# Scores of the attention blocks as one matmul of 64 rows by 128 columns in place of four of 64 by 32

## The chip, the cores and the metric

The kernel runs on one core of one Trainium2 chip. The metric is the device time of one execution in microseconds (us). A change is called faster or slower in this document where it moves the time by more than 0.2%.

## The reference

A transformer layer with attention and a dense block side by side. x is 2048 tokens of 512, float32.

```
xn  = layernorm(x)
q, k, v = split(xn @ wqkv)                    # 32 heads of 16
o   = softmax(q @ k.T / 4) @ v                # per head, 2048 x 2048 scores
out = x + o @ wo + gelu(xn @ w1 + b1) @ w2 + b2     # w1 is 512 x 1792
```

## The kernel before

**Stages.** A prologue (to about 87 us) normalizes x, turns it, and makes q and k of the first eight heads, most of v, and the scores of the first 19 units. Its order on every engine is set by a small planner (`Plan`). Then the block loop runs (to about 1425 us): 512 units, a unit being four heads, 512 queries and 128 keys. A short tail finishes the output.

**A unit** has two halves, `a` = 0 and 1 in `unit` (L819). In each half TensorE gets, in this order:

- two products of *transposed scores* (`e_half`, L432, tile pT: keys x queries) and two of *scores* (`s_half`, L405, tile pS: queries x keys), in the order pT, pS, pS, pT. One pT and one pS use rows 0 to 63 of the array, the other two rows 64 to 127, since a head's q and k are stacked with their low halves into 64 rows (62 used for the scores). Each product is of 64 rows by 128 columns of weights, and 512 columns of moving operand. ScalarE takes the exponential of pT (`pe`, L443). VectorE takes the row maxima of pS (`mt`, L402), which are needed for blocks to come: after the 16 units of a stretch they are turned by two matmuls of 64 rows by 32 columns (`m_turn`, L378), go to memory and come back as two more rows of the stacked q;
- four matmuls with v (`v_half`, L446, tile pV), float32, 64 rows by 32 columns each, one per head, in one half of the array's rows;
- three or four *dense* products (tile pD) in the other half of the rows: projections, the two layers of the dense block and the output projection, cut into such pieces. `dense` hands them out, and their number per half comes from a pace per group (`FAST`, `MEAN`, `SLOW`).

The next half swaps the halves of the rows. Scores run 19 units ahead of the transposed scores (`LEAD`).

**How a product becomes matmuls.** `tiled` (L202) cuts the 128 columns of weights of a score, transposed score or dense product into pieces of `wide[0]` columns, each written to its own 32 partitions of the PSUM bank. `wide[0]` is 128 while the prologue's plan is made, and 32 after that, so the block loop's pieces are all of 64 rows by 32 columns. `user` is "D" for dense products of the block loop, and None for scores. Dense products that take a score's place in the last 19 units (`Halves`, L767) pass None too. The matmuls with v call `product` without `tiled`. Where the array is used whole (prologue, tail), `nc.tensor.matmul` is called directly.

**Order.** The block loop's order on each engine is the order in which the code issues it. PSUM has three banks for pS, three for pT, one each for pV and pD.

Of the kernel before, what the change touches and what calls it, by code (L numbers as in the profile page):

```python
# [18 lines left out]
P = 128  # L19
# [26 lines left out]
VT = 2600, -8000  # L46
WV_TAIL, WV_DVE = 56000, 2
FINE = "fine"
ORDERED = {mybir.EngineType.SP, mybir.EngineType.PE, mybir.EngineType.Activation, mybir.EngineType.DVE, mybir.EngineType.Pool}
GELU_C = 0.7978845608028654  # L50
GELU_A = 0.044715
# [7 lines left out]
def layer_kernel(ctx: ExitStack, tc: tile.TileContext, x, wqkv, wo, w1, b1, w2, b2, out):  # L59
# [68 lines left out]
    def scales(am, n, bank, box):  # L128
# [9 lines left out]
        nc.vector.tensor_scalar(c[:, :n], pb[:, :n], 2.0 ** -100, 2.0 ** 100, op0=ALU.max, op1=ALU.min)  # L138
        yield FINE
        fac = const.tile([P, n], F32, name=f"fac{len(made)}")  # L140
        inv = const.tile([P, n], F32, name=f"inv{len(made)}")
        made.append(fac)
        nc.vector.tensor_single_scalar(fac.bitcast(I32), c[:, :n].bitcast(I32), 0x7F800000, op=ALU.bitwise_and)
        yield FINE
        nc.vector.reciprocal(inv, fac)
# [26 lines left out]
    def product(user, *args, **kw):  # L172

        p = nc.tensor.matmul(*args, **kw)  # L174
        if user is None:
            return
        if user in goal:
            p._wait_ge(turns[user], counted[user])
            tc.declare_fence(p.ins, group=goal.pop(user))
        newest[user] = p  # L180
# [19 lines left out]
    wide = [32]  # L200

    def tiled(user, dst, lhs, rhs, start, stop):  # L202

        for j in range(0, P, wide[0]):
            product(user, dst[j:j + wide[0]], lhs[:, j:j + wide[0]], rhs, start=start, stop=stop)


    scale_of, wfs = {}, []
# [177 lines left out]
    def s_mm(u, n, s):  # L386

        t, i = divmod(u, 16)
        g, qb = divmod(t, NQB)
        qt, kb = divmod(i, 4) if t else (i % 4, i // 4)  # L390
        ks, qs = kst[g % 2], qst[g % 2]
        p, a = divmod(n, 2)
        r = slice(64 * a, 64 * a + 62)
        tiled(None, s, qs[qb][r, p, P * qt:P * qt + P], ks[kb][r, p, :], True, True)
# [37 lines left out]
    def e_half(u, n):  # L432

        p, a = divmod(n, 2)
        t, kt = divmod(u, 16)
        g, qb = divmod(t, NQB)
        st = banks("T")
        r = slice(64 * a, 64 * a + 64)
        k0 = (kt % 4) * P
        tiled(None, st, kst[g % 2][kt // 4][r, p, k0:k0 + P], qst[g % 2][qb][r, p, :], True, True)  # L440
        pe = work.tile([P, QB], F32, name="pe", bufs=12)
        ptiles[u, n] = pe
        nc.scalar.activation(pe, st, AF.Exp, scale=scale_of[g // 2])  # L443
        given("act", 520)
# [131 lines left out]
    class Group:  # L576
# [15 lines left out]
        def product(self, side):  # L592

            if self.bank is None:
                self.bank, self.key = self.alloc()
            lhs, rhs = self.prods[side % 2][self.at[side % 2]]()
            start = self.first and self.at == [0, 0]
            if side == 2:
                self.at = [min(self.at[0] + 1, n) for n in self.n]
                nc.tensor.matmul(self.bank, lhs, rhs, start=start, stop=self.last and self.over())  # L600
                return
            r = slice(64 * side, 64 * side + 64)
            self.at[side] += 1
            tiled("D", self.bank, lhs[r], rhs[r], start, self.last and self.over())
# [34 lines left out]
    def by_slots(gen):  # L639

        def step():
            w = FINE
            while w == FINE:
                w = next(gen, 0)
            if w is None:
                later(1, step, True)
# [226 lines left out]
    with ExitStack() as st1:  # L873
# [40 lines left out]
        loads, fac_v, ready_w = [None] * NM, [], {}  # L914
        ctx.enter_context(tc.manual_schedule(engines=ORDERED))
        plan = Plan(xs=8, xp=8, stg=3, pf=2, wch=3, wq=2, S=4, X=4)
# [354 lines left out]
        for n, src in enumerate(every[:NM]):  # L1271
            key = ("wch", "m", n)
            dst = am_all[:, 12 + n:13 + n] if n < 2 else am_all[:, n - 2:n - 1] if n < 9 else amx[:, n - 2:n - 1]
# [346 lines left out]
```

## Time and profile before

| | us |
|---|---|
| median of 3 runs | 1438.83 (1438.03 to 1439.07) |
| the profiled execution | 1438.07 |
| its span, first to last instruction | 1436.3 |
| TensorE busy, 39979 matmuls | 1423.7 |
| weight loads busy, 39979 | 969.1 |
| VectorE busy | 1346.9 |
| ScalarE busy | 1253.5 |
| GpSimd busy | 693.4 |

Engines are named PE (matmuls), PEld (weight loads, which can run beside matmuls), DVE (VectorE), ACT (ScalarE), POOL (GpSimd) and SP. In a row of the timeline stand the start, the time from the first start to the last end, the engine, the line, the operation, the tiles out<-in, the shapes and the number of records that are merged. A record of a matmul is modelled from its start and its size, so that the next may start well before it ends: steps are read from start to start. The four strips of one product are four records that overlap. The granted clock of TensorE is 1.00 throughout.

### The profile page before, as it was taken

The page shows a single profiled execution, that of the slowest core. Times are in us where ns is not written, and L with a number is a line of the kernel's source. Part 1 is how long each engine was busy: PE and PEld are TensorE (multiplying, and loading weights), DVE is VectorE, ACT ScalarE, POOL GpSimd, SP SyncE. Part 2 cuts the span into 40 slices and gives each one's busy share as a digit, 9 for nine tenths or more (in the row PEclk, how much of TensorE's full clock was granted, in tenths as well). Part 3 has the DMA queues.
Part 4 walks back from the last instruction along what each step waited for, and adds up shares of the span by engine and source line. Part 5 has one row for each costly group of instructions (what it writes and reads, how often), then busy time and mean ns, then how long its engine had stood idle before and what let it go on. Part 6 is the DMA issues. An engine that isn't in the chain of part 4 may idle for free.

```text
span 1436.3 us, 88274 instructions
## 1 busy us (share of the span) xinstructions
PE 1423.7 (99%) x39979; PEld 969.1 (67%) x39979; DVE 1346.9 (94%) x2239; ACT 1253.5 (87%) x2389; POOL 693.4 (48%) x780
## 2 busy tenths in 40 slices
PE   8999999999999999999999999999999999999998
PEld 4657777666667777666667766676666667666665
DVE  8989999999999999999999999999999999999943
ACT  6678888889999888999988899998889998888886
POOL 6203866665687311478831157783026787202210
PEclk9999999999999999999999999999999999999999
DMA  7733556455224111221122011122112110212323
GB/s 233 225 114 97 162 158 206 158 172 148 85 65 128 60 27 27 64 76 43 38 59 75 25 51 45 52 71 60 38 32 77 57 39 19 60 56 78 109 73 116
DMA packets 110784, 124.95 MB, mean 87 GB/s; under 512 B 20812, under 2 KB 82252, under 8 KB 110408
## 3 DMA queue, kind: packets, MB, share of 16 engines
q1 hardware_dynamic: 103208, 109.87, 25.1%
q10 hardware_dynamic: 7200, 9.44, 2.2%
q8 instruction: 312, 5.11, 1.5%
q14 instruction: 64, 0.52, 0.1%
HBM read 81.79 MB, written 37.34 MB: 83 GB/s over the span
## 4 chain that ended last, share of the span: by engine, by line
PE 90%; DVE 5%; DMA 2%; issue 2%; ACT 1%; POOL 0%; SPq 0%; DVEq 0%; ACTq 0%; POOLq 0%
PE pD L174 28%; PE pV L174 26%; PE pT L174 19%; PE pS L174 16%; DVE mt L402 3%; DMA wch<-in_B_w_dram 1%; DMA pe<-in_A_x_dram 0%; DVE bs L1011 0%; DMA qk_d<-stg 0%; DMA wq<-in_A_wqkv_dram 0%; DMA wch<-in_A_wo_dram 0%; DVE ac L1493 0%; PE pD L1074 0%; ACT pe L443 0%; DVE wvh L1196 0%
## 5 line engine op out<-in xcount | busy, mean ns | idle before, releaser
L402 DVE TENSOR_REDUCE mt<-pS 128x1 f32<-128x512 f32 x2029 | 1279.1, 683 | 34.7 <-PE pS L174 8.2
L443 ACT ACTIVATE pe<-pT 128x512 f32<-128x512 f32 x2048 | 1109.4, 599 | 141.0 <-PE pT L174 60.2
L174 PE MATMUL pV<-pe,vv 64*32 64x512 f32 x8192 | 1086.6, 591 | 0.1
L174 PE MATMUL pT<-qst,kst 64*32 64x512 f16 x8192 | 703.4, 378 | 0.6 <-ACT vv L1212 0.3
L174 PE MATMUL pS<-kst,qst 62*32 62x512 f16 (+1 forms) x7945 | 627.0, 378 | 1.3 <-issue 0.8
L174 PEld LDWEIGHTS <-qst 62*32 62x32 f16 (+1 forms) x7964 | 309.9, 91 | 186.0 <-issue 34.1
L174 PE MATMUL pD<-xb,wc 64*32 64x512 f16 x5376 | 363.3, 375 | 0.0
L174 PE MATMUL pD<-w_s,g 64*32 64x512 f16 x5376 | 361.1, 375 | 0.0
L174 PEld LDWEIGHTS <-kst 64*32 64x32 f16 x8192 | 281.3, 91 | 98.5 <-issue 24.4
L174 PEld LDWEIGHTS pV<-pe,vv 64*32 64x32 f32 x8192 | 241.5, 105 | 11.0 <-PE pV L174 2.3
L174 PEld LDWEIGHTS <-wc 64*32 64x32 f16 x5376 | 160.4, 91 | 45.2 <-issue 0.3
L174 PEld LDWEIGHTS <-g 64*32 64x32 f16 x5376 | 162.6, 91 | 38.8 <-POOL g L1408 0.3
L174 PE MATMUL pD<-xt,wqk_h 64*32 64x512 f16 x2400 | 160.0, 376 | 0.1
L372 POOL TENSOR_SCALAR mparts<-mx 128x16 f16<-128x16 f32 x32 | 6.6, 206 | 294.3 <-DVE mx L370 284.6
L1460 POOL TENSOR_TENSOR xa<-xa,yt 128x512 f32<-128x512 f32 x16 | 20.6, 1284 | 167.8 <-ACT yt L1458 167.8
L174 PEld LDWEIGHTS <-wqk_h 64*32 64x32 f16 (+1 forms) x2448 | 78.2, 92 | 20.3 <-issue 1.0
L1414 POOL TENSOR_TENSOR t<-t,hh 128x512 f32<-128x512 f32 x56 | 71.9, 1284 | 4.7
L1407 POOL TENSOR_TENSOR t<-t,hh 128x512 f32<-128x512 f32 x56 | 71.8, 1283 | 4.5
L1412 POOL TENSOR_TENSOR t<-hh 128x512 f32<-128x512 f32 x56 | 58.3, 1041 | 21.3 <-ACT hh L1435 18.9
L1409 POOL TENSOR_TENSOR g<-t,g 128x512 f16<-128x512 f32 x56 | 65.2, 1165 | 4.7
L174 PE MATMUL pD<-wo_s,oc 64*32 64x512 f16 x912 | 61.0, 376 | 0.3 <-issue 0.3
L513 POOL TENSOR_TENSOR osb<-osb,rb 128x512 f32<-128x512 f32 x31 | 39.9, 1286 | 42.3 <-DMA rb<-den_d 29.0
(170 smaller groups left out, 942.1 us busy)
## 6 DMA issues: line engine op xcount, KB each, us to landing
wc<-w_d SPq DMA_DIRECT2D x56, 256.0 KB
qk_d<-stg SPq DMA_DIRECT2D x32, 256.0 KB
rb<-den_d SPq DMA_DIRECT2D x124, 64.0 KB
wch<-in_B_w_dram ACTq DMA_DIRECT2D x14, 512.0 KB
wch<-in_B_w_dram SPq DMA_DIRECT2D x28, 256.0 KB
w_d<-wsp SPq DMA_DIRECT2D x28, 256.0 KB
kst<-qk_d SPq DMA_DIRECT2D x64, 96.0 KB
qst<-qk_d SPq DMA_DIRECT2D x64, 96.0 KB
```

The costliest lines, as they stand in the source:

```text
L174: p = nc.tensor.matmul(*args, **kw)
L372: lambda: nc.gpsimd.tensor_scalar(parts[:, :, 0], mx[:, 0], 1.0 / MROW, 0.0, op0=ALU.mult, op1=ALU.add),
L402: nc.vector.reduce_max(mt_of[t][:, n // 2 + n % 2 * 2, qt, kb:kb + 1], s, axis=AX.X)
L443: nc.scalar.activation(pe, st, AF.Exp, scale=scale_of[g // 2])
L513: pooled((1280, lambda: nc.gpsimd.tensor_tensor(osb, osb, rb, op=ALU.mult)), (620, lambda: nc.gpsimd.tensor_scalar(ot[:, 0], osb, 1.0, 0.0 ...
L1407: (1280, lambda: nc.gpsimd.tensor_tensor(t1, t1, hh, op=ALU.mult)),
L1409: (1160, lambda: nc.gpsimd.tensor_tensor(g[:, 1, f, :], t1, g[:, 0, f, :], op=ALU.subtract)),
L1412: pooled((1040, lambda: nc.gpsimd.tensor_tensor(t1, hh, hh, op=ALU.mult)), (620, lambda: nc.gpsimd.tensor_scalar(t1, t1, 1.0, 1.0 / GELU_A ...
L1414: (1280, lambda: nc.gpsimd.tensor_tensor(t1, t1, hh, op=ALU.mult)),
L1460: add = lambda: nc.gpsimd.tensor_tensor(xa, xa, yt, op=ALU.add)
```

## The change

`tiled` takes the larger of `wide[0]` and an entry for the user. Scores and transposed scores (user None) thus become one matmul of 64 rows by 128 columns in the block loop as well; dense products ("D") and those with v keep 32.

```diff
+WIDE = {None: 128}
...
     def tiled(user, dst, lhs, rhs, start, stop):
 
-        for j in range(0, P, wide[0]):
-            product(user, dst[j:j + wide[0]], lhs[:, j:j + wide[0]], rhs, start=start, stop=stop)
+        n = max(wide[0], WIDE.get(user, 0))
+        for j in range(0, P, n):
+            product(user, dst[j:j + n], lhs[:, j:j + n], rhs, start=start, stop=stop)
```

Lines after the first addition move by one, those after `tiled` by two. On VectorE, ScalarE, GpSimd and SP the instructions stand in the same order as before. On TensorE the same products stand in the same order, with fewer instructions.

TensorE before, the end of a dense group's products and the scores of a half in the middle of the block loop (each row of the scores stands there four times; kst and qst are the stacked k and q, wc is a part of w1, xb of the normalized x):

```order
L174 MATMUL pD_22326<-xb_15758,wc_21822 32x512
...
L174 LDWEIGHTS kst1_3_86
L174 MATMUL pT_22390<-qst1_1_92,kst1_3_86 32x512
...
L174 LDWEIGHTS qst1_3_94
L174 MATMUL pS_22397<-kst1_0_83,qst1_3_94 32x512
...
L174 MATMUL pS_22404<-kst1_0_83,qst1_3_94 32x512
...
L174 MATMUL pT_22410<-qst1_1_92,kst1_3_86 32x512
L174 MATMUL pV_21341<-pe_22252,vv_95 32x512
```

TensorE after, at such a place of the block loop (32x512 and 128x512 are partitions and columns of the result):

```order
L175 MATMUL pD_15833<-xb_12170,wc_15466 32x512
L175 LDWEIGHTS kst1_3_86
L175 MATMUL pT_15885<-qst1_0_91,kst1_3_86 128x512
L175 LDWEIGHTS qst1_1_92
L175 MATMUL pS_15889<-kst1_3_86,qst1_1_92 128x512
L175 LDWEIGHTS qst1_1_92
L175 MATMUL pS_15892<-kst1_3_86,qst1_1_92 128x512
L175 LDWEIGHTS kst1_3_86
L175 MATMUL pT_15895<-qst1_0_91,kst1_3_86 128x512
L175 MATMUL pV_15174<-pe_15777,vv_95 32x512
```

Sixteen pairs of a weight load and a matmul have become four, and every half now goes from 32 columns to 128 and back. The instructions of TensorE are 64460 rows before and 40034 after.

TensorE after, where the row maxima of a stretch are turned (mparts are the maxima, nident the negative identity), in the scores of the second half of a stretch's first unit:

```order
L175 MATMUL pS_2258<-kst0_0_79,qst0_2_89 128x512
L380 LDWEIGHTS mparts_2209
L380 MATMUL pT_2261<-nident_98,mparts_2209 32x64
...
L175 LDWEIGHTS kst0_3_82
L175 MATMUL pT_2269<-qst0_0_87,kst0_3_82 128x512
L175 MATMUL pV_1415<-pe_2176,vv_95 32x512
```

The two turning matmuls keep 32 columns; before, their neighbours had 32 as well, now they stand between matmuls of 128. There are 32 such places, the first of them in the prologue, where the neighbours had 128 already. In the whole program the pieces of successive matmuls go from 64x128 to 64x32 1058 times (twice before), and from 64x32 to 64x128 1056 times (once before).

## The prediction

> **What bounds the kernel now.** I read the page first (engines, then the chain that ended last), then the groups of instructions with their shapes kept apart, then single stretches of the timeline.
>
> ```profile
> PE 1423.7 (99%) x39979; PEld 969.1 (67%) x39979; DVE 1346.9 (94%) x2239; ACT 1253.5 (87%) x2389; POOL 693.4 (48%) x780
> PE 90%; DVE 5%; DMA 2%; issue 2%; ACT 1%; POOL 0%; SPq 0%; DVEq 0%; ACTq 0%; POOLq 0%
> ```
>
> TensorE is busy 99% of the span and 90% of the chain runs through it. Work per time there is the question, and busy shares don't answer it, since eight matmuls run beside each other. So I count half units. A half unit is one turn of the inner loop of `unit`: two products of scores, two of transposed scores, then four matmuls with v beside three or four dense products. The group of the matmuls with v, taken from 200 to 1400 us alone, gives the period:
>
> ```profile
> L174 PE MATMUL pV<-pe,vv 64*32 64x512 f32 x7384 | 979.6, 591 | 0.1
> ```
>
> Each of the four matmuls of a half leaves two records (float32 goes through in two passes), so 7384 records are 923 halves in 1200 us: 1.300 us per half. There are 1024 halves in the kernel (512 blocks, two each), 1331 us of the 1438.
>
> What is in a half? Two stretches of the timeline. The shape after the operands is rows*columns of the weights, then of the moving operand; the second number is the time from the first start to the last end of the merged records.
>
> ```profile
> 77.86 0.37 PE L174 MATMUL pD<-wvh,xt 64*128 64x512 f16 x1
> 77.89 0.37 PE L174 MATMUL pT<-wvh,xt 64*128 64x512 f16 x1
> 78.07 0.37 PE L174 MATMUL pD<-wvh,xt 64*128 64x512 f16 x1
> ...
> 78.29 0.38 PE L174 MATMUL pD<-wvh,xt 64*128 64x512 f16 x1
> 78.32 0.37 PE L174 MATMUL pT<-wvh,xt 64*128 64x512 f16 x1
> 78.62 0.20 PE L378 MATMUL pS<-nident,mparts 64*32 64x64 f16 x2
> 78.76 0.61 PE L174 MATMUL pT<-wvh,xt 64*128 64x512 f16 x4
> 701.41 0.61 PE L174 MATMUL pV<-pe,vv 64*32 64x512 f32 x3
> ...
> 701.84 0.60 PE L174 MATMUL pV<-pe,vv 64*32 64x512 f32 x3
> ```
>
> The first stretch is of the prologue, where scores and v tiles are already made by weights of 64 rows by 128 columns. In one half of the rows a 512-column fp16 matmul follows the other after 0.215 us (77.86, 78.07, 78.29), while the other half of the rows runs its own. A pass with v takes 0.43 us (701.41 to 701.84). A half of the block loop therefore streams for at least 2 x 0.215 + 2 x 0.43 = 1.29 us where the matmuls with v stand. It takes 1.300. TensorE streams back to back, whatever the number of instructions that carry the stream. VectorE stands close behind:
>
> ```profile
> 62.52 1.88 DVE L402 TENSOR_REDUCE mt<-pS 128x1 f32<-128x512 f32 x3
> 64.31 0.68 DVE L402 TENSOR_REDUCE mt<-pV 128x1 f32<-128x512 f32 x1
> 575.79 12.14 DVE L402 TENSOR_REDUCE mt<-pS 128x1 f32<-128x512 f32 x20
> ```
>
> Unhindered, a row maximum follows the last one after 0.60 us (62.52 to 64.31 is three; twenty at 575.79 are as tight). Two of them per half make 1.20 us, the lowest that a half can come to whatever happens on TensorE.
>
> **The change part by part.** It removes, in each half, 12 of the 16 weight loads and 12 of the 16 matmuls of scores; no column of the stream goes away, because four matmuls over four strips of 32 columns run beside each other and stream as long as one over 128. What the fewer instructions save is bounded by what the weight loads of scores waited for "issue", the time for which the profile shows no cause:
>
> ```profile
> L174 PEld LDWEIGHTS <-qst 62*32 62x32 f16 x7888 | 304.4, 91 | 181.4 <-issue 33.1
> L174 PEld LDWEIGHTS <-kst 64*32 64x32 f16 x8192 | 281.3, 91 | 98.5 <-issue 24.4 <-DMA qst<-m_d 0.7
> ```
>
> That is 33.1 + 24.4 = 57.5 us at most, and nothing at least. I take nothing, because the half already stands 0.01 us above its stream.
>
> What it adds is a change of the array's division. Before, everything in the block loop used pieces of 64 rows by 32 columns. Now each half goes from 64x32 (v and dense) to 64x128 (scores) and back: two changes in each of 1024 halves. The trace of before shows that very pair once each way, in the rows at 78.32, 78.62 and 78.76 above, where the two small turning matmuls of L378 stand between wide ones. From the last wide start to the small one is 0.30 us in place of 0.215; from the small one, 64 columns and so 0.027 us of stream at the same rate, to the next wide one 0.14 us. That is 0.09 and 0.11 us over the stream. That this was no wait for data shows in the weight loads and the instruction that made their data:
>
> ```profile
> 78.07 0.13 PEld L174 LDWEIGHTS <-xt 64*128 64x128 f16 x2
> 78.62 0.09 PEld L378 LDWEIGHTS <-mparts 64*32 64x32 f16 x2 [0.42 <-issue]
> 78.75 0.33 PEld L174 LDWEIGHTS <-xt 64*128 64x128 f16 x6
> 77.78 0.22 POOL L374 TENSOR_TENSOR mparts<-mx,mparts 128x16 f16<-128x16 f32 x1
> ```
>
> The turned data were there at 78.00. A load is otherwise issued as soon as the matmul ahead of it starts (78.07 beside 78.07); this one stood until 78.62, and the wide one behind it until 78.75. Other changes of the row division cost alike:
>
> ```profile
> 46.20 0.81 PE L1074 MATMUL pT<-xt,wqk_h 128*128 128x512 f16 x3
> 46.94 0.60 PE L174 MATMUL pS<-kst,qst 62*128 62x512 f16 x3
> 30.36 0.60 PE L1044 MATMUL pT<-ident,xs 128*128 128x128 f32 x4
> 30.90 0.39 PE L174 MATMUL pS<-kst,qst 62*128 62x512 f16 x1
> ```
>
> Three at 0.215 put the last full-array start at 46.63, and the next follows 0.31 later: 0.09 over. Behind float32 the four transposes (0.11 apart) put the last at 30.69, and the wide one comes 0.21 later: 0.10 over. One pair of rows speaks the other way, a change in the column division alone:
>
> ```profile
> 8.60 0.27 PE L972 MATMUL pT<-ident,amq 128*2 128x128 f32 x1 [0.26 <-ACT wqk_h L959]
> 8.70 0.59 PE L1279 MATMUL pS<-wo_s 128*128 128x512 f16 x2
> 8.60 0.20 PEld L1279 LDWEIGHTS <-wo_s 128*128 128x128 f16 x2
> ```
>
> From 2 columns to 128 took 0.11 us, the plain step of such a transpose, and the weights came early. So a change costs between 0 and, if the next load waited for the modelled end of the matmul before it (0.38 us of record, then 0.09 of load, against a step of 0.215), 0.25 us. I take 0.10, from the rows at 78.62 and 78.76, which are of the same shapes. The Trainium skill, page "TensorEngine Tiling (Array Packing)", section "Key Properties", says that changing the tiling mode, not just the tile, drains TensorE. By it, each of these changes pays; by the rows at 8.60, not each does; at 78.62 the trace agrees with it. It gives no price. The page "TensorE: Matmul & The Clock Gate", section "Step-by-step: what each phase is for", puts the drain at about 128 cycles, which at its 2.4 GHz is an estimate of 0.053 us a change; the sum below would then come to some 1560 us. The trace has 0.09 to 0.11, and that decides.
>
> A third, small loss: with 64x32 pieces the strips of one product start up to 0.04 us after each other (701.41 x3 lasts 0.61 where one record has 0.591), and today the next product of each strip simply follows on it. A change waits for the last strip; 0.02 us per half.
>
> So a half becomes 1.29 + 2 x 0.10 + 0.02 = 1.51 us, 0.21 over 1.300. Times 1024 that is 215 us. The lead that one half of the rows has today where only three dense products stand beside v is lost too; it is in the 1.300 already, since 1.51 counts the longer side.
>
> The turning matmuls keep 32 columns and now stand between wide ones, once in each of the 31 stretches after the prologue:
>
> ```profile
> L378 PEld LDWEIGHTS <-mparts x64: 88/88/90, 78.6 to 1377.0; 64*32 64x32 f16 x64
> 124.62 0.24 PE L378 MATMUL pT<-nident,mparts 64*32 64x64 f16 x2
> 124.72 0.40 PE L174 MATMUL pT<-qst,kst 64*32 64x512 f16 x4
> ```
>
> Today they take 0.10 us (124.62 to 124.72). With a change on each side they take what they took at 78.32: 0.30 + 0.14 = 0.44. 31 x 0.34 = 10.5 us.
>
> The last 19 units put the output products into the places of the scores, and those go wide with them; they are among the 1024 halves. Every other engine has its instructions in the same order, and its work is spread over longer halves: VectorE needs 1.20 of 1.51, ScalarE 87% of what is now 1.30. DMA has more time too. The moves of SP and POOL cost nothing under that cover; were it gone, they would have to pass 1.51 us a half, and nothing in the page comes near it.
>
> Sum against the profiled execution (1438.07 us, span 1436.3): 1438.07 + 215 + 10.5 = 1663.6. The median of the runs is 0.8 higher, so I predict **1664 us**, 16% slower.
>
> **The rivals.** *Dividing only the columns anew is free, and fewer instructions help* (the other side, faster). For it: the rows at 8.60, and that the halves of rows stay as they are. Against it: 78.62 and 78.76. It would give back at most the 57.5 us, so 1381; VectorE's 1.20 us sets a bottom of 1438 - 1024 x 0.10 = 1336 under that. I put it midway, 1410. It decides below 57.5 / 2048 = 0.028 us per change; above that the changes outweigh any saving. Chance 0.08.
>
> *No cost and no gain*: the four strips ran beside each other anyway, and TensorE's stream sets the half in both kernels: 1438. Chance 0.03. What a measurement of this kernel can tell from no change is about 0.2%, 3 us.
>
> *A dearer change.* If each waits for the modelled end and a fresh load, 0.25 us: 1024 x 2 x 0.15 more than forecast, 1971; with half of that 1817. For it: v's passes are the longest records (0.591), and no row shows 64x32 behind them. Against it: the float32 row at 30.90, 0.10. Chance 0.09.
>
> **How the numbers follow.** The forecast has 0.80: 1664, with a change of 0.07 to 0.13 us its own range is 1664 -+ 61, 1603 to 1725. I widen that to 1590 to 1750, for a cheaper or dearer change still near the rows; out of it fall the free change and most of the dearer one. Slower 0.80 + 0.09 = 0.89, same 0.03, faster 0.08.
>
> **What would show it.** Right: about 923 x 1.30 / 1.51 = 795 halves (6360 records of v) in 1200 us of the block loop; first starts of scores 0.30 us after the last dense start, weight loads standing for "issue" at both borders of a half, VectorE near 85% busy (0.68 + 0.60 us of records in 1.51) and waiting for pS. Wrong: loads of kst and qst that begin while dense matmuls still start, and a half at 1.30 or under; or borders of 0.45 us and a half near 1.8.

## The result, and the profile after

The changed kernel takes 1695.77 us (median of three, 1693.59 to 1698.59) against 1438.83: 17.9% slower, ratio 1.179 with a 95% interval of 1.176 to 1.182. The profiled execution is the slowest of the three, 1698.59 us with a span of 1696.8.

The page of the changed kernel, engines and chain:

```profile
PE 1685.9 (99%) x27766; PEld 503.8 (30%) x27766; DVE 1377.5 (81%) x2239; ACT 1268.7 (75%) x2389; POOL 691.7 (41%) x780
PE 74%; ACT 21%; DMA 2%; DVE 1%; issue 1%; SPq 0%; POOL 0%; ACTq 0%; DVEq 0%; POOLq 0%
```

12,213 matmuls and as many weight loads fewer, and TensorE is as "busy" as before, 99%: a record of a matmul lasts 0.38 us whether its successor follows at once or not, and eight overlap, so the union of the records hides a stall of 0.1 us. VectorE fell from 94% to 81%, ScalarE from 87% to 75%; the same work in a longer span. The chain now shows 21% ScalarE; a run below asks whether that means anything.

The groups of the changed kernel from 200 to 1400 us, then of the whole span, are plainer:

```profile
L175 PE MATMUL pV<-pe,vv 64*32 64x512 f32 x6188 | 821.9, 601 | 0.0
```

```profile
L175 PE MATMUL pT<-qst,kst 64*128 64x512 f16 x2048 | 627.5, 383 | 1.4 <-ACT vv L1214 1.4
L404 DVE TENSOR_REDUCE mt<-pS 128x1 f32<-128x512 f32 x2029 | 1306.8, 686 | 251.5 <-PE pS L175 251.3
L175 PEld LDWEIGHTS <-kst 64*128 64x128 f16 x2048 | 118.9, 94 | 517.8 <-issue 515.3
```

6188 records of v are 773.5 halves in 1200 us, 1.551 us each; before it was 1.300. The 0.251 us more, times 1024 halves, are 257 us, all of the difference. VectorE now waits 251 us for pS; before, its group stood idle for 35 in all. And the weight loads of kst stood 515 us for "issue", where before it was 24. That is the mark of the change at one of its two borders: a load that nothing in the profile holds up, and that doesn't start. At the other border the profile puts it down to the v matmuls.

One half of the changed kernel on TensorE, and the place where the row maxima are turned:

```profile
700.51 0.60 PE L175 MATMUL pV<-pe,vv 64*32 64x512 f32 x3
...
701.06 0.39 PE L175 MATMUL pT<-qst,kst 64*128 64x512 f16 x1
701.06 0.60 PE L175 MATMUL pS<-kst,qst 62*128 62x512 f16 x2
701.29 0.38 PE L175 MATMUL pT<-qst,kst 64*128 64x512 f16 x1
701.59 0.63 PE L175 MATMUL pV<-pe,vv 64*32 64x512 f32 x4
701.62 0.61 PE L175 MATMUL pD<-xb,wc 64*32 64x512 f16 x8
702.05 0.60 PE L175 MATMUL pV<-pe,vv 64*32 64x512 f32 x3
...
702.59 0.39 PE L175 MATMUL pT<-qst,kst 64*128 64x512 f16 x1
```

```profile
632.75 0.38 PE L175 MATMUL pS<-kst,qst 62*128 62x512 f16 x1
633.05 0.20 PE L380 MATMUL pS<-nident,mparts 64*32 64x64 f16 x2
633.19 0.39 PE L175 MATMUL pT<-qst,kst 64*128 64x512 f16 x1
633.50 0.63 PE L175 MATMUL pV<-pe,vv 64*32 64x512 f32 x4
```

A half's two score waves (a wave is one pT and one pS beside each other) start 0.23 us apart (701.06 to 701.29). From there to v it is 0.30, from v's first pass to its second 0.46, and to the next scores 0.54: 1.53 us. Stream alone would be 0.215, 0.215, 0.43 and 0.43. At the turning matmuls the steps are 0.30 and 0.14.

### The profile page after: what moved, and what is told of

Same layout as the page of the kernel before. It is cut to its first block, busy times and chain, and to the rows that moved or that the text cites. A ratio compares the mean times of both kernels' runs of the same rounds, so it can differ in the third digit from the quotient of the medians.

```text
span 1696.8 us, 62839 instructions
## 1 busy us (share of the span) xinstructions
PE 1685.9 (99%) x27766; PEld 503.8 (30%) x27766; DVE 1377.5 (81%) x2239; ACT 1268.7 (75%) x2389; POOL 691.7 (41%) x780
## 4 chain that ended last, share of the span: by engine, by line
PE 74%; ACT 21%; DMA 2%; DVE 1%; issue 1%; SPq 0%; POOL 0%; ACTq 0%; DVEq 0%; POOLq 0%
PE pV L175 24%; PE pT L175 21%; ACT pe L445 19%; PE pD L175 19%; PE pS L175 10%; ACT hh L1437 1%; DMA wch<-in_B_w_dram 1%; ACT t L1403 1%; DMA pe<-in_A_x_dram 0%; DMA qk_d<-stg 0%; DVE bs L1013 0%; DMA wch<-in_A_wo_dram 0%; DMA wq<-in_A_wqkv_dram 0%; PE pT L380 0%; ACT yt L1460 0%
## 5 line engine op out<-in xcount | busy, mean ns | idle before, releaser
L404 DVE TENSOR_REDUCE mt<-pS 128x1 f32<-128x512 f32 x2029 | 1306.8, 686 | 251.5 <-PE pS L175 251.3
L175 PE MATMUL pT<-qst,kst 64*128 64x512 f16 x2048 | 627.5, 383 | 1.4 <-ACT vv L1214 1.4
L175 PE MATMUL pS<-kst,qst 62*128 62x512 f16 x2029 | 609.2, 382 | 0.7 <-DMA qst<-qk_d 0.4
L175 PEld LDWEIGHTS pV<-pe,vv 64*32 64x32 f32 x8192 | 158.4, 105 | 415.4 <-PE pV L175 395.0
L175 PEld LDWEIGHTS <-kst 64*128 64x128 f16 x2048 | 118.9, 94 | 517.8 <-issue 515.3
L175 PEld LDWEIGHTS <-g 64*32 64x32 f16 x5376 | 105.9, 92 | 68.9 <-issue 5.1
L175 PEld LDWEIGHTS <-wc 64*32 64x32 f16 x5376 | 103.3, 92 | 63.2 <-issue 5.1
L175 PEld LDWEIGHTS <-qst 62*128 62x128 f16 x2048 | 111.3, 94 | 5.8 <-issue 1.7
L175 PEld LDWEIGHTS <-wqk_h 64*32 64x32 f16 (+1 forms) x2448 | 52.8, 92 | 35.0 <-issue 2.1
```

The lines of the kernel that those rows point to most:

```text
L404: nc.vector.reduce_max(mt_of[t][:, n // 2 + n % 2 * 2, qt, kb:kb + 1], s, axis=AX.X)
```

## The experiments

The theory: each change of the array's division makes TensorE wait until all that runs has ended, before it even loads the next weights, and costs about 0.1 us. The rivals: the wide products themselves are slow; one half of the rows no longer gets ahead of the other; ScalarE's exponentials have become the bound; a change of the columns alone is free where all 128 rows are used. The kernel before took 1436.06, 1436.90 and 1438.85 us beside these runs.

### The change without the wide products, and its control

```diff
# in e_half of the kernel before, ahead of the scores (control: 32 for 128, twice)
+        if n in (1, 2):
+            nc.tensor.matmul(st[:128, :64], kst[g % 2][kt // 4][r, p, k0:k0 + 128], qst[g % 2][qb][r, p, :64], start=True, stop=True)
         tiled(None, st, kst[g % 2][kt // 4][r, p, k0:k0 + P], qst[g % 2][qb][r, p, :], True, True)
```

> The kernel before, with one small matmul of 64 rows by 128 columns (64 moving columns) put ahead of the first transposed scores of each half, into the bank that the scores then overwrite; all real products keep 32 columns. So there are two changes of the array's division per half and no wide product. Theory (each change costs about 0.1 us): a half of 1.30 becomes 1.52 to 1.56, 1024 halves: 1665 to 1700 us. Rival (wide score products or their weight loads are what is slow): about 1440 to 1470, the small matmul's own stream. Rival (ScalarE's exponentials set the period of the changed kernel): 1440 to 1470 too.

> The control to the marked kernel: the same small matmul with 64 rows by 32 columns, so that no division changes. All theories: 1439 to 1470 us (0.03 us of stream in one strip of a half, 1024 times, where nothing hides it). If it comes near 1680, it was the extra matmul and not the change that cost in the marked kernel.

Measured: 1688.78 us with the wide mark, 1446.27 with the narrow one. Every real product is as before in both. TensorE with the wide mark:

```profile
700.68 0.20 PE L441 MATMUL pT<-qst,kst 64*128 64x64 f16 x1
700.81 0.40 PE L174 MATMUL pT<-qst,kst 64*32 64x512 f16 x4
700.82 0.60 PE L174 MATMUL pS<-kst,qst 62*32 62x512 f16 x8
701.05 0.39 PE L174 MATMUL pT<-qst,kst 64*32 64x512 f16 x4
701.26 0.60 PE L174 MATMUL pV<-pe,vv 64*32 64x512 f32 x4
...
701.69 0.60 PE L174 MATMUL pV<-pe,vv 64*32 64x512 f32 x4
...
702.23 0.20 PE L441 MATMUL pT<-qst,kst 64*128 64x64 f16 x1
```

From the mark, 0.03 us of stream, to the first score it takes 0.13. From the scores to v, where no division changes now, 0.21, the plain step; v's first pass takes 0.43. And from v's second pass to the next mark 0.54, as to the wide scores of the changed kernel. The two changes moved to other borders, and the cost moved with them. (1688.78 - 1446.27) / 2048 = 0.118 us for a change, with all that hangs on it. One wide matmul of 64 moving columns per half makes the kernel 253 us slower (1688.78 against 1436.06), nearly as much as the changed kernel's four of 512 do. The rival of slow wide products falls. Nor do fewer instructions help in any way that shows: the changed kernel has far fewer than this one, and is no faster.

### Half as many wide products, twice as many changes

```diff
# kernel before, tiled with a parameter n=0 and max(wide[0], n); in e_half alone
-        tiled(None, st, kst[g % 2][kt // 4][r, p, k0:k0 + P], qst[g % 2][qb][r, p, :], True, True)
+        tiled(None, st, kst[g % 2][kt // 4][r, p, k0:k0 + P], qst[g % 2][qb][r, p, :], True, True, P)
```

> Only the transposed scores are made by 128 columns, the scores keep 32: half as many wide products as in the changed kernel, but four changes per half in place of two, since the order is pT, pS, pS, pT. Theory (changes cost): three score waves with a change behind each (0.31, 0.33, 0.31) and the stretch with v and dense products of 0.86 + 0.05 + 0.09: a half of 1.94 us, 2050 to 2150 us in all, slower than with both wide. Rival (wide products cost, each by itself): half of the loss, about 1567.

Measured: 2125.63 us. TensorE in one half:

```profile
700.44 0.63 PE L174 MATMUL pV<-pe,vv 64*32 64x512 f32 x4
...
701.43 0.39 PE L174 MATMUL pT<-qst,kst 64*128 64x512 f16 x1
701.75 0.41 PE L174 MATMUL pS<-kst,qst 62*32 62x512 f16 x8
702.09 0.39 PE L174 MATMUL pT<-qst,kst 64*128 64x512 f16 x1
```

pT, pS and pT stand apart by 0.32 and 0.34. One pT used rows that pS beside it leaves free, and still ran alone: two score waves became three. Undoing half of the change costs 430 us more than the whole change. The steps from the first scores to v are 0.32, 0.34 and 0.32 us, 0.45 more than the 0.23 and 0.30 of the changed kernel. Of that, 0.215 is the stream of the third wave, and the other 0.24 are the two more changes. So the changes decide, by their own price and by the work that they keep apart, and not the number of wide products.

### Pieces of 64 columns

```diff
-WIDE = {None: 128}
+WIDE = {None: 64}
```

> Scores and transposed scores by pieces of 64 columns in place of 128: as many changes as in the changed kernel, each product two pieces. Theory (a change costs whatever it changes to): 1690 to 1705 us, as with 128. Rival (the width of the pieces costs, by longer weight loads or all four strips having to be free): clearly less, 1500 to 1620.

Measured: 1712.92 us, 8 us over what I had expected and 17 over the changed kernel. A change costs no less where it changes less. The 17 us are 0.017 per half, and they stand between the two score waves, which start 0.25 us apart in place of 0.23:

```profile
700.70 0.40 PE L175 MATMUL pT<-qst,kst 64*64 64x512 f16 x2
700.95 0.38 PE L175 MATMUL pT<-qst,kst 64*64 64x512 f16 x2
```

That they are the start of a second piece is not shown. It may be the width: in the run of fillers below, the step behind a piece of 64 columns is longer as well, though no second piece stands there.

### One half of each unit alone

```diff
# kernel before with the parameter n of tiled; in s_mm and in e_half
+        ..., True, True, P if n < 2 else 0)
```

> Wide scores and transposed scores in the first half of each unit alone; the second half keeps 32 columns. Theory (changes cost): 512 halves of 1.54 us as in the changed kernel and 512 of about 1.30; the turning matmuls stand in the second half and pay no change: 1436 + 512 x 0.24 = 1559, from 1545 to 1580 us. If what costs is the lost lead of one half of the rows, which a change in every other half already takes away, it comes nearer to the changed kernel: over 1600.

Measured: 1546.60 us, 110 over the kernel beside it for half of the changes. The changed kernel is 257 us over, and 247 without some 10 for the turning matmuls, which pay nothing here; half of that is 123. So half of the changes cost a little less than half of the loss, 0.107 us for each; where the 13 us went is not shown. The rival, by which the time would be over 1600, falls: the lost lead adds nothing to be seen.

### Dense products by 128 columns too

```diff
-WIDE = {None: 128}
+WIDE = {None: 128, "D": 128}
```

> Dense products by 128 columns as well, v alone keeps 32: still two changes per half, but v and the dense products, which use different halves of the rows, now differ in division. Theory (a change waits for the whole array, whatever rows the next matmul uses): v and dense run one after the other, a half of 0.54 + 0.90 + 0.09 + 0.77 = 2.30 us less what the next scores overlap: 2350 to 2480 us. Rival (a change holds up its own rows alone): v and dense still run beside each other, 1600 to 1720 us.

Measured: 2467.79 us. TensorE over one half:

```profile
701.46 1.06 PE L175 MATMUL pV<-pe,vv 64*32 64x512 f32 x8
702.45 0.39 PE L175 MATMUL pD<-xb,wc 64*128 64x512 f16 x1
702.47 0.39 PE L175 MATMUL pS<-kst,qst 62*128 62x512 f16 x1
702.68 0.38 PE L175 MATMUL pD<-xb,wc 64*128 64x512 f16 x1
702.69 0.38 PE L175 MATMUL pT<-qst,kst 64*128 64x512 f16 x1
702.89 0.38 PE L175 MATMUL pD<-xb,wc 64*128 64x512 f16 x1
703.11 0.38 PE L175 MATMUL pT<-qst,kst 64*128 64x512 f16 x1
703.33 0.38 PE L175 MATMUL pS<-kst,qst 62*128 62x512 f16 x1
703.63 1.06 PE L175 MATMUL pV<-pe,vv 64*32 64x512 f32 x8
```

As many changes as in the changed kernel, and 772 us more. The first dense product uses the rows that v leaves free; it waits for both passes of v. Behind it dense products and scores of one division run beside each other in pairs at 702.45 and 702.68. So a change waits for the whole array. The Trainium skill, page "TensorEngine Tiling (Array Packing)", section "Key Properties", says that the switch of the mode drains TensorE; the trace agrees, and adds that the other rows are drained too.

### More work for ScalarE

The chain of the changed kernel goes through `pe` (ScalarE) for 19% of the span. Its end, at 701.04, and the next scores, at 701.06, stood 0.02 us apart, which looks like a wait:

```profile
699.95 1.09 ACT L445 ACTIVATE pe<-pT 128x512 f32<-128x512 f32 x2 [0.45 <-PE pS L175]
```

```diff
# the changed kernel, in e_half
         nc.scalar.activation(pe, st, AF.Exp, scale=scale_of[g // 2])
+        if n in (1, 2):
+            nc.scalar.activation(spare_t, ident[:, :64], AF.Copy)
```

> The changed kernel with one more small ScalarE instruction (a copy of 128 x 64, about 0.2 us) behind one exponential of each half. The chain of the changed kernel goes through the exponentials for 19% of the span; if they set its period, 1024 x 0.2 more: about 1900 us. Theory (TensorE's changes set it, and the exponential's end only falls beside the next start): ScalarE's 75% takes it, 1690 to 1705 us.

Measured: 1693.50 us, no more than the changed kernel. ScalarE of this run, and TensorE beside it:

```profile
701.04 0.60 ACT L446 ACTIVATE pe<-pT 128x512 f32<-128x512 f32 x1 [0.16 <-PE pS L176]
701.53 0.25 ACT L448 ACTIVATE spare_t<-ident 128x64 f32<-128x64 f32 x1
701.68 0.59 ACT L446 ACTIVATE pe<-pT 128x512 f32<-128x512 f32 x1
```

```profile
702.16 0.39 PE L176 MATMUL pT<-qst,kst 64*128 64x512 f16 x1
```

The exponential now ends at 702.27, and the next pT started at 702.16. Nothing waited for it. In the changed kernel the two merely fell together, and the chain, which takes the last event before a start for its cause, followed the wrong one.

### Which changes cost

The prediction's rival rested on one pair of rows, a change among 128 rows that seemed free. The prologue of the kernel before fills waiting time with matmuls whose result nothing uses; here they go through eight divisions.

```diff
+        FILLS = ((128, 128), (128, 32), (128, 64), (128, 128), (64, 128), (64, 32), (64, 64), (64, 128))
...
-                    nc.tensor.matmul(wp, wo_s[:, 0, 0, 0:P], wo_s[:, 0, 0, :], start=True, stop=True)
+                    h, n = FILLS[fills[0] % len(FILLS)]
+                    fills[0] += 1
+                    nc.tensor.matmul(wp[:n], wo_s[:h, 0, 0, 0:n], wo_s[:h, 0, 0, :], start=True, stop=True)
```

> The kernel before, in whose prologue the 49 filling matmuls of zeros, which compute nothing that is used, go through eight divisions in turn: 128 rows by 128, 32, 64 and 128 columns, then 64 rows by 128, 32, 64 and 128. It is read from the steps in the trace, each against 0.215 us for 512 columns at the full clock; the time stays at that of the kernel before. Theory (every change of the division costs alike, 64 rows or 128): 0.31 us at each. Rival (with 128 rows a change of the columns alone is free, as the rows at 8.60 of the kernel before suggest, and only with 64 rows it costs): 0.22 us at the changes among 128 rows, 0.31 at those among 64 and between.

Measured: 1451.19 us, 12 over the kernel beside it, which I had not expected (last section). Weight loads of the fillers, first at half the clock, where 512 columns stream in 0.43 us (the step of the fillers in the first 5 us of the kernel before), then at the full one:

```profile
5.01 0.10 PEld L1284 LDWEIGHTS <-wo_s 64*128 64x128 f16 x1 [0.44 <-issue]
5.55 0.10 PEld L1284 LDWEIGHTS <-wo_s 128*128 128x128 f16 x1 [0.44 <-issue]
6.09 0.10 PEld L1284 LDWEIGHTS <-wo_s 128*32 128x32 f16 x1 [0.43 <-issue]
6.63 0.13 PEld L1284 LDWEIGHTS <-wo_s 128*64 128x64 f16 x1 [0.44 <-issue]
7.20 0.10 PEld L1284 LDWEIGHTS <-wo_s 128*128 128x128 f16 x1 [0.44 <-issue]
7.74 0.10 PEld L1284 LDWEIGHTS <-wo_s 64*128 64x128 f16 x1 [0.44 <-issue]
```

```profile
23.44 0.09 PEld L1284 LDWEIGHTS <-wo_s 128*32 128x32 f16 x1 [0.60 <-issue]
23.76 0.11 PEld L1284 LDWEIGHTS <-wo_s 128*64 128x64 f16 x1 [0.23 <-issue]
24.10 0.33 PEld L1074 LDWEIGHTS <-wqk_h 128*128 128x128 f16 x3 [0.23 <-issue]
```

Steps of 0.54 to 0.57 at half the clock, at least 0.11 over the stream; 0.32 and 0.34 at the full one, 0.10 and 0.13 over. It makes no difference whether rows or columns change; only behind a piece of 64 columns is the step 0.02 to 0.03 longer. The rival falls. Why the step behind the two-column transpose of the kernel before was free stays open. A like transpose with one column of weights is followed by a matmul of 128 by 128 after 0.11 us in the kernel before (22.34 to 22.45), but by one of 64 by 32 after 0.20 in this run (32.60 to 32.80). That fits a transpose that keeps the division of the whole array however few columns it uses; it is argued and not shown.

## Why the prediction was right

- **The bound and its stream: right.** TensorE set the period in both kernels, and no column of stream went away: 4 products of scores took two waves before and after.
- **A change costs what the few rows of the prologue showed: right.** The steps of 0.30 and 0.14 us around one pair of turning matmuls came back at each pair of them, and the 0.30 between scores and v in every half.
- **Its size: a little too small.** I had 0.10 for each change and 0.02 for the strips' lag, 0.22 a half over a stream of 1.29. In the half shown at 701 the four steps lie 0.24 over it: the second score wave 0.015, v 0.085, v's second pass 0.03 and the next scores 0.11. The waves right behind a change, 0.23 and 0.46 for 0.215 and 0.43, were no term of mine. A half with four dense products beside v, as from 705.67 to 707.21, takes 0.01 more again. The marked kernel's 0.118 us for a change is the whole price, against 0.10 plus half of 0.02 in my sum. A half came to 1.551, of which the turning matmuls are 0.010; I had 1.51. The 0.031 us left over, times 1024, are the 32 us by which 1664 falls short of 1696.
- **The turning matmuls: right.** They stand between a pS and a pT that otherwise start together, and hold these 0.44 us apart (632.75 to 633.19). From that I took off the 0.10 that they cost before, read at one place.
- **The lead of the shorter side is lost and needs no term: right.** The half shown at 701 has three dense products beside v, others four; it lasts as long as v either way.
- **Fewer instructions save nothing: right as far as runs show.** With the narrow mark 1024 matmuls more cost 10 us; nothing came back in the changed kernel.
- **The signs: right but for one border.** I had 795 halves in 1200 us, and 773.5 came; VectorE is at 81% for 85. The loads stand for "issue" ahead of the scores alone; ahead of v the profile puts the wait to the v matmuls.
- **The faster rival: fell.** Its rows were real, but the change between 64 by 32 and 64 by 128 costs the 0.118 us of the marked kernel, far above the 0.028 at which that rival decided, and the fillers show changes among 128 rows at the common price.
- **The dearer rival: fell.** It had 0.25 us over the stream for a change; the borders are 0.085 and 0.11 over. Float32 ahead of a change costs 0.09 like the others, if the strips' lag of 0.02 is taken off 0.11.

No version beat the kernel before. Every one that adds changes is slower, and the block loop of the kernel before has none.

## What to carry to other kernels

Before cutting a product differently, look at what its neighbours on TensorE use: in these runs, going from one division of the array to another cost 0.11 to 0.12 us each time, however small the matmul and whichever rows it used, and work of different divisions no longer ran side by side. Fewer, larger matmuls saved nothing here, where the strips already ran beside each other. A busy share of 99% says nothing of it; a step from start to start does, and one odd neighbour in the old trace can hold the price.

## What the runs showed of the hardware that was not expected

The granted clock fell to half for some 7 us in the profiled execution of the changed kernel, after TensorE had waited 1.4 us for the last rows of q. Stretches of its start, with the granted clock in the third column from the end:

```profile
88.00:92.00 4.00, 2.62 (x29) 0.74 (x26) 1.97 (x4) 3.58 (x7) 0.00 (x0) 1.00 0.38 121
92.00:94.00 2.00, 2.00 (x20) 0.44 (x16) 1.49 (x5) 1.09 (x2) 0.00 (x0) 0.58 0.01 4
94.00:98.00 4.00, 4.00 (x35) 0.79 (x36) 1.65 (x3) 1.48 (x3) 0.00 (x0) 0.50 0.00 0
98.00:100.00 2.00, 2.00 (x29) 0.69 (x29) 1.08 (x3) 0.69 (x2) 0.00 (x0) 0.71 0.00 0
```

It happened 2 us after the wait, while scores and dense products already ran. In the run with more work for ScalarE, else the same on TensorE, the clock stayed at 1.00 there and the time was 5 us lower. What made it fall is not shown: TensorE waited as long, 1.38 us from 31.8, in the run with dense products by 128 columns, and 2.2 us from 140.3 in the one with the narrow mark, and the clock stayed at 1.00.

With a change behind each filling matmul, the steps stayed at those of half the clock from the start to 19 us, though one matmul followed the other; in the kernel before, fillers of one division go from 0.43 to 0.22 us a step 5 us after the start. The half clock is read from these steps alone: the column of the granted clock shows 1.00 in the first stretches of both runs. In the run of fillers, 16 transposes of one division stood from 19.4 to 22.9 us, most of them 0.21 us apart where the kernel before has 0.11, and from 23.4 us on the steps were those of the full clock. Later, after a wait of 1.4 us that ended at 43.5, the clock fell once more: the granted clock from 43.8 to 47.3 us is 0.51.

The first product of q and k came 10.6 us late (24.10 for 13.49). Of that, the 35 fillers ahead of it, at 0.11 for a change, are an estimate of 4 us, and the half clock has most of the rest. Behind the second fall the first product of v was 12.0 us late (48.35 for 36.30), which are the 12 us of that run.

The Trainium skill, page "TensorE: Matmul & The Clock Gate", section "What's actually happening", has the clock rise after some 3.4 us of sustained activity. The 3.5 us of transposes shortly ahead of the rise fit it. But a stream with a drain of 0.11 us in every 0.54 did not raise the clock for 18 us, so the measurement and the page differ if such a stream counts as sustained; whether it was the drains or the narrower pieces that kept the activity too low was not tried.
